# The first expert's list and the end of the last expert, in a kernel of retention, eight experts and a rational two-layer block

## The chip, the core and the metric

The kernel runs on one core of a Trainium2 chip. The metric is the device time of one execution in microseconds. Engines are called as in the profile: PE is TensorE's products and PEld its weight loads, DVE is VectorE, ACT is ScalarE, POOL is GpSimd, SP is SyncE, which here only issues transfers.

## The reference, cut to what matters

Three stages follow each other. N = 4608 tokens (8 x 576), width 512 (8 heads x 64), 8 experts of inner width 1024, a last block of inner width 2048.

```python
ret = (q @ k.T / 8) * gamma[h] ** (i - j), causal;   x = ret @ v        # retention, 8 heads
do_compute = x @ w_skip > 0                                             # router
e_idx = argmax(x[do_compute] @ w_gate);  gate_w = softmax value of e_idx
x[tokens of e] += gate_w * (relu(x @ w1[e]) @ w2[e])                    # eight experts
h = x @ w_in                                                            # last block
P = a0 + a1*h + a2*h*h + a3*h*h*h
Q = 1 + |b0|*|h| + |b1|*h*h
out = (P / (Q + 1e-6)) @ w_out
```

## The kernel before, in words

Products run with operands split in a high and a low part (two float32r halves), three products for one; 12 products of 512 columns make one inner tile. Work is written in an order by hand: under `manual_schedule` each engine gets its instructions in the order in which the Python code emits them, and waits only for semaphores. The change moves code, so it moves instructions on every engine.

*Stage 1* (to about 235 us) does the retention and the router over 36 token tiles. The router writes, by indirect DMA on POOL, each token's number into the list of its expert in DRAM (`XI`), and a list `PM` that puts 1024 tokens in an order in which the first 512 hold none of the last expert's. Then comes a branch (`spill`, L596) for experts with more than 336 tokens, which isn't taken here; all engines pass it.

*Stage 2* (to about 530 us) goes through the eight experts. `lists` (L661) loads an expert's list into `idx`, `gather` (L676) fetches its tokens' rows from `Z` in DRAM by three indirect DMAs, `turn_e` transposes them on PE (L694), with the high part cast on ACT (L695) and the low part on DVE (L696). Expert e has eight steps: steps 0 to 3 are `up` (L722, 24 products of 336 columns each), steps 4 to 7 are `down` (L743, 18 output products each). After the last one DVE adds the sums to the tokens (L748), and `scatter` (L759) writes them back to `Z` on POOL. `feed` moves the weights through 8 slots: SP loads them into one of three `raw` buffers (L112, L116, and L110 for the last block's second matrix, slots 64 to 71), ACT casts the high part (L127), DVE subtracts the low part (L131). The load for slot s waits until the low part of slot s - 3 has been read. Ahead of the first expert, PE runs 20 products whose result isn't used (`spin`, L501).

*Stage 3* works on nine blocks of 512 tokens. A block's rows come by `fetch` (SP; block 0 and block 1 by indirect DMAs of POOL, `fetch_at`, L685), are transposed (`turn_f` for block 0, `turn_b` for the others, one PSUM buffer for the latter), and then run through 16 steps. Step n has: `head` (12 products L774 on PE into one of three PSUM buffers `h`; five operations on ACT, L781 to L785; two on POOL, L786 and L787), `quot` (three on DVE: L798 product with `h`, L799 reciprocal, L800 the quotient), `parts` (ACT cast L805, POOL low part L806) and `back` (12 products L907 into the block's four output sums). In the steady order, step n emits head n, parts n - 2, quotient n, back n - 4. In steps 5 to 8 of block 0 the last two weight slots are split in halves (`part_rest`, L941 and L942). The four buffers `gt` that hold the split quotients begin with two `raw` buffers, those of the last weights.

What sets the order around the change: the list's load is in ACT's queue; in the last expert the block's transposes stand in steps 5 and 6, heads 0 and 1 behind the third output group, and the last expert's scatter behind head 2.

Of the kernel before, what the change touches and what calls it, by code (L numbers as in the profile page):

```python
# [17 lines left out]
N, DM = B * S, H * D  # L18
# [13 lines left out]
NBLK = N // TB  # L32
NF2 = F2 // P
LAG = 4
SPIN = (10, 20)
NQ = 2 * TB // P
OOB = 1 << 20
TINY = 2.0 ** -15
# [39 lines left out]
def body(nc, tc, a, out):  # L78
# [577 lines left out]

    gap = nblk[0:1, E + 1:E + 2]

    def lists(e0, e1):
        for e in range(e0, e1):  # L660
            nc.scalar.dma_start(out=idx[:, e], in_=XI[e * RR:e * RR + NC3 * P, :].rearrange("(c p) t -> p c t", p=P))  # L661
        if e1 == E:
            nc.scalar.dma_start(out=pidx, in_=PM.rearrange("(c p) t -> p c t", p=P))

# [14 lines left out]
                bounds_check=N - 1, oob_is_err=False), "get", ["put"])  # L679


    def fetch_at(j):
        nc.gpsimd.memset(gap, 0)
        for c in range(TB // P):
            ins = nc.gpsimd.indirect_dma_start(  # L685
                out=d2[:, c, :], out_offset=None, in_=Z[:, :],
                in_offset=bass.IndirectOffsetOnAxis(ap=pidx[:, j * (TB // P) + c, 0:1], axis=0),
                bounds_check=N - 1, oob_is_err=False)
            if j == 0:
                apart(ins, "first", [])  # L690
# [101 lines left out]
    def head(j, f):  # L792
        el[j, f] = act(j, f)

    def quot(j, f):
        ps, p, q = el[j, f]
        V = nc.vector
        V.scalar_tensor_tensor(out=ps, in0=p, scalar=ab[:, 1:2], in1=ps, op0=ALU.add, op1=ALU.mult)  # L798
        V.reciprocal(out=q, in_=q)  # L799
        V.scalar_tensor_tensor(out=p, in0=ps, scalar=ab[:, 0:1], in1=q, op0=ALU.add, op1=ALU.mult)  # L800

    def parts(j, f):
        p = el.pop((j, f))[1]
# [4 lines left out]

    order = ExitStack()
    order.enter_context(tc.manual_schedule())  # L810
    spin(ps_h.tile([P, DM], F32, tag="h", name="spin"), win[0][:, 0], SPIN[1])
    lists(0, 1)
    gather(0)
    feed(4, 4)
    for c in range(NC3):
        turn_e(0, c)
    feed(0)
    while nxt["raw"] < 6:
        load_raw(nxt["raw"])
# [3 lines left out]
    for e in range(E):  # L823
        for i in range(8):
            s = 8 * e + i
            if i == 1:
                gather(e + 1) if e + 1 < E else fetch_at(0)
            if s == 3:
                lists(2, E)
            if i < 4:  # L830
                up(e, i)
                if i == 0 and e > 0:
                    scatter(e - 1)
            else:
                if e + 1 == E and i in (5, 6):
                    if i == 5:
                        cvx.close()
                        el_p = ctx.enter_context(tc.tile_pool(name="el", bufs=2, reuse_waits="tile"))
                        pq.append(tuple(el_p.tile([P, TB], F32, name=nm + "0", bufs=1) for nm in "pq"))
                    turn_f(2 * i - 10)  # L840
                    turn_f(2 * i - 9)
                elif e + 1 < E and i < 4 + NC3:
                    turn_e(e + 1, i - 4)
                down(e, i - 4)
                if e + 1 == E and i == 6:
                    feed(NSLOT - 2)
                    feed(0)
                    head(0, 0)
                    quot(0, 0)
                    head(0, 1)  # L850
            feed(5 + s + min(max(s - 58, 0), 3), NSLOT - 2)
            K = 2 * (NCV - NCA) + 2
            for ph in range(*(min(max(x - 6, 0) * K // 54, K) for x in (s, s + 1))):
                n = NCA + ph // 2
                if ph % 2 == 0:
                    cv(conv_load, n + 1, NCA, NCV)
                    cv(conv_abs, n, NCA, NCV)
                    cv(conv_words, n, NCA, NCV)
                    cv(conv_hi, n - 1, NCA, NCV)
                else:  # L860
                    cv(conv_add, n, NCA, NCV)
                    cv(conv_lo, n - 1, NCA, NCV)
    quot(0, 1)
    gt = [pool["raw"].tile([P, 1024], F32, tag="raw", name="raw")[:, :].bitcast(F32R)
          .rearrange("p (h t) -> p h t", h=2) for _ in range(2)]
    parts(0, 0)
    head(0, 2)
    scatter(E - 1)
    quot(0, 2)
    mo.close()  # L870
    right.close()

# [11 lines left out]
    os = {}  # L884

    def fetch(j):
        if j == 1:
            fetch_at(j)
            return
        for c in range(NTB):  # L890
            r = j * TB + c * P
            nc.sync.dma_start(out=d2[:, c, :], in_=Z[r:r + P, :])
# [53 lines left out]
    for n in range(3, M + LAG):  # L946
        if n < M:
            j, f = steps[n]
            if f == 5 and j + 1 < NBLK:
                fetch(j + 1)  # L950
            at = TB_AT if j else (11, 12, 13, 14)
            if f in at and j + 1 < NBLK:
                turn_b((j + 1) * NTB + at.index(f))
            head(j, f)
            for x in late:
                put_at(*x)
            late.clear()
        if n < M + 2:
            parts(*steps[n - 2])
        if n < M:  # L960
            quot(j, f)
        if 5 <= n < 5 + len(rest):
            part_rest(n - 5)
        if n >= LAG:
            back(*steps[n - LAG])
# [32 lines left out]
```

## Time and profile before

| what | us |
|---|---|
| three runs: median (lowest, highest) | 1346.33 (1341.47, 1347.14) |
| the profiled execution | 1344.77 |
| its span, first to last instruction | 1342.8 |
| TensorE busy in the span | 1297.7 (97%) |
| VectorE, ScalarE, GpSimd busy | 1074.2, 793.5, 786.9 |
| mean granted TensorE clock, as a share of the full one | 0.984 |
| one indirect gather on POOL, busy, and the pause after it | 1.0 and 0.3 |

A matmul that waits on a pipeline still counts as busy, so the share of 97% says little; the waits of PE and the granted clock in each stretch say where time can go. The clock has two levels here, 1.0 (2.4 GHz) and 0.5 (1.2 GHz). In the timeline an entry is a run of instructions of one line; the number in brackets is the idle time of its engine before it and what ended that wait.

### The profile page before, as it was taken

To read this page: it belongs to the slowest core of one execution; us is meant where nothing else is said; L and a number is where in the kernel's file an instruction comes from. 1 tells how busy PE (TensorE), PEld (TensorE's weight loads), DVE (VectorE), ACT (ScalarE), POOL (GpSimd) and SP (SyncE) were. 2 spreads that over 40 slices of the span, in tenths; PEclk is the share of its full clock that TensorE was granted. 3 is DMA by queue.
4 is the path that set the end of the run, shared out by engine and by line. 5 is a ranking of instruction groups with operands and counts; after the bars stand their busy time and mean duration, and the time that the engine had idled before them with its cause. 6 is when DMAs were issued, how large, how long until landed. Compare 5 with 4: busy or idle time off the path is not lost.

```text
span 1342.8 us, 20351 instructions
## 1 busy us (share of the span) xinstructions
PE 1297.7 (97%) x7615; PEld 1087.7 (81%) x7615; DVE 1074.2 (80%) x1140; ACT 793.5 (59%) x1379; POOL 786.9 (59%) x666
## 2 busy tenths in 40 slices
PE   8999998799999998989999999999999999999998
PEld 6887887688888886868888888888888888888886
DVE  3786886367777776888798898888888888888885
ACT  3564664244444445666676777666676676766764
POOL 3466565223333332866777777676666666666774
PEclk8999999799999999989999999999999999999999
DMA  9999993367666764100200101001010010010000
GB/s 213 251 212 210 245 250 92 92 201 220 217 222 223 233 222 145 52 1 1 63 1 29 35 1 63 0 6 59 1 63 1 1 63 1 23 40 1 32 1 31
DMA packets 160555, 128.16 MB, mean 95 GB/s; under 512 B 87930, under 2 KB 127610, under 8 KB 160448
## 3 DMA queue, kind: packets, MB, share of 16 engines
q1 hardware_dynamic: 149248, 111.71, 30.4%
q0 software_dynamic: 6272, 13.73, 3.0%
q10 hardware_dynamic: 4928, 1.34, 0.5%
q8 instruction: 61, 1.00, 0.3%
q14 instruction: 46, 0.38, 0.1%
HBM read 99.35 MB, written 28.93 MB: 96 GB/s over the span
## 4 chain that ended last, share of the span: by engine, by line
PE 84%; DVE 6%; issue 3%; DMA 3%; POOL 2%; ACT 1%; SPq 1%; POOLq 0%; ACTq 0%; DVEq 0%
PE h L774 27%; PE o L907 27%; PE y L743 9%; PE h L722 8%; PE xp L373 2%; PE ot L335 2%; PE ot L330 2%; PE sc L314 2%; PE t L694 2%; DVE q L799 2%; PE st L352 1%; PE tp L291 1%; PE tp L304 1%; DMA c<-in_moe_w_out 1%; DMA lk<-in_k 1%
## 5 line engine op out<-in xcount | busy, mean ns | idle before, releaser
L799 DVE RECIPROCAL q<-q 128x512 f32<-128x512 f32 x142 | 476.0, 3352 | 74.1 <-POOL q L787 74.1
L786 POOL TENSOR_TENSOR p<-p,h 128x512 f32<-128x512 f32 x142 | 183.9, 1295 | 164.3 <-ACT p L782 164.2
L774 PE MATMUL h<-d,wi 128*128 128x512 f32 x960 | 236.0, 396 | 5.3 <-DVE d L800 3.0
L787 POOL TENSOR_TENSOR q<-q,s 128x512 f32<-128x512 f32 x142 | 184.1, 1297 | 66.0 <-ACT s L785 59.3
L774 PEld LDWEIGHTS h<-d,wi 128*128 128x128 f32 x960 | 181.2, 190 | 43.9 <-DVE d L800 3.5
L781 ACT COPY h<-h 128x512 f32<-128x512 f32 x144 | 85.1, 591 | 211.9 <-PE h L774 211.9
L907 PE MATMUL o<-w,raw 128*128 128x512 f32 x864 | 207.8, 389 | 0.1
L907 PE MATMUL o<-w,g 128*128 128x512 f32 x864 | 207.6, 389 | 0.0
L907 PEld LDWEIGHTS o<-w,raw 128*128 128x128 f32 x864 | 162.2, 188 | 34.2 <-POOL raw L806 0.5
L907 PEld LDWEIGHTS o<-w,g 128*128 128x128 f32 x864 | 162.0, 188 | 34.0 <-POOL g L806 0.2
L774 PE MATMUL h<-xb,wi 128*128 128x512 f32 x768 | 186.5, 392 | 0.0
L774 PEld LDWEIGHTS h<-xb,wi 128*128 128x128 f32 x768 | 143.0, 188 | 29.4
L743 PE MATMUL y<-w,hr 128*128 128x512 f32 (+1 forms) x576 | 139.2, 397 | 0.0
L782 ACT ACTIVATE p<-h,ab 128x512 f32<-128x512 f32 x142 | 111.4, 785 | 45.1 <-POOL g L806 28.4
L722 PE MATMUL h<-d,w 128*128 128x336 f32 x768 | 121.9, 320 | 1.8 <-DVE hr L727 1.3
L722 PEld LDWEIGHTS h<-d,w 128*128 128x128 f32 x768 | 120.4, 191 | 3.4 <-DVE hr L727 1.8
L743 PEld LDWEIGHTS y<-w,hr 128*128 128x128 f32 (+1 forms) x576 | 98.9, 175 | 29.6
L785 ACT ACTIVATE s<-s,ab 128x512 f32<-128x512 f32 x144 | 119.2, 828 | 0.0
L798 DVE SCALAR_TENSOR_TENSOR h<-p,ab,h 128x512 f32<-128x512 f32 x142 | 106.0, 747 | 14.9 <-POOL p L786 14.9
L800 DVE SCALAR_TENSOR_TENSOR p<-h,ab,q 128x512 f32<-128x512 f32 x142 | 106.7, 751 | 5.0
L185 POOL TENSOR_TENSOR cr<-cr,cy 128x256 f32<-128x256 f32 x32 | 24.8, 775 | 136.8 <-DVE cr L178 96.1
L127 ACT CAST w<-raw 128x1024 fp32r<-128x1024 f32 x70 | 73.4, 1048 | 53.1 <-DMA raw<-in_moe_w 30.8
(129 smaller groups left out, 1844.5 us busy)
## 6 DMA issues: line engine op xcount, KB each, us to landing
raw<-in_moe_w SPq DMA_DIRECT2D x62, 512.0 KB, 4.2
Z<-xs SPq DMA_DIRECT2D x36, 256.0 KB, 4.3
lk<-in_k SPq DMA_DIRECT2D x32, 256.0 KB, 5.5
lv<-in_v SPq DMA_DIRECT2D x32, 256.0 KB, 5.9
c<-in_moe_w_in SPq DMA_DIRECT2D x16, 512.0 KB, 6.4
c<-in_moe_w_out SPq DMA_DIRECT2D x31, 256.0 KB, 4.6
d<-Z SPq DMA_DIRECT2D x28, 256.0 KB, 3.7
out<-d SPq DMA_DIRECT2D x27, 256.0 KB, 2.4
```

What stands on the lines that cost most here:

```text
L722: nc.tensor.matmul(out=ps, lhsT=w[:, pw, k, ff * P:(ff + 1) * P], rhs=xp[e][:, px, k, :], start=(n == 0), stop=(n == 11))
L743: nc.tensor.matmul(out=ys[e][c][0:cnt[c]], lhsT=h[:, ph, c * P:c * P + cnt[c]], rhs=w[:, pw, ff, :], start=(i == 0 and ff == 0 and j == 0) ...
L774: nc.tensor.matmul(out=ps, lhsT=w[:, pw, k, o:o + P], rhs=xb[j][:, px, k, :], start=(n == 0), stop=(n == 11))
L781: S.copy(out=h, in_=ps)
L782: S.activation(out=p, in_=ps, func=A.Identity, scale=ab[:, 3:4], bias=ab[:, 2:3])
L785: S.activation(out=s, in_=s, func=A.Identity, scale=ab[:, 5:6], bias=ab[:, 6:7])
L786: G.tensor_tensor(out=p, in0=p, in1=h, op=ALU.mult)
L787: G.tensor_tensor(out=q, in0=q, in1=s, op=ALU.add)
L798: V.scalar_tensor_tensor(out=ps, in0=p, scalar=ab[:, 1:2], in1=ps, op0=ALU.add, op1=ALU.mult)
L799: V.reciprocal(out=q, in_=q)
L800: V.scalar_tensor_tensor(out=p, in0=ps, scalar=ab[:, 0:1], in1=q, op0=ALU.add, op1=ALU.mult)
L907: nc.tensor.matmul(out=os[j][c], lhsT=g[:, pg, c * P:(c + 1) * P], rhs=w[:, pw, f % 2, :], start=(f == 0 and i == 0), stop=(f == NF2 - 1 a ...
```

## The change

1. The first expert's list is loaded from SP's queue (`lists(0, 1, nc.sync)`), and three of the unused products follow each of the first expert's three transpose groups.
2. In the last expert the transposes of block 0 move from steps 5 and 6 to steps 4 and 5, head 0 goes ahead of the third output group (step 6), and the last eight weight casts are spread: the step's own `feed` no longer runs ahead, and the rest follows quotient 1. The scatter comes before quotient 1, head 2 ahead of the last parts.
3. The quotient is cut in two: `quot_a` is L798, `quot_b` the reciprocal and the last operation. In step n, `quot_b` of n - 1 is emitted ahead of head n and `quot_a` of n after parts. What is emitted between them on DVE (a weight half, the low part of a transpose) now lies between the two.
4. The four gathers of block 1 go one by one into steps 5 to 8, and its transposes into steps 9, 11, 13 and 14 instead of 11 to 14.

```diff
-SPIN = (10, 20)
+SPIN = (10, 20, 3)
...
-    def lists(e0, e1):
+    def lists(e0, e1, eng=nc.scalar):
         for e in range(e0, e1):
-            nc.scalar.dma_start(out=idx[:, e], in_=XI[...])
+            eng.dma_start(out=idx[:, e], in_=XI[...])
...
-    def fetch_at(j):
-        nc.gpsimd.memset(gap, 0)
-        for c in range(TB // P):
+    def fetch_at(j, cs=range(TB // P)):
+        if cs[0] == 0:
+            nc.gpsimd.memset(gap, 0)
+        for c in cs:
...
-    def quot(j, f):
+    def quot_a(j, f):
+        ps, p, q = el[j, f]
+        nc.vector.scalar_tensor_tensor(out=ps, in0=p, scalar=ab[:, 1:2], in1=ps, op0=ALU.add, op1=ALU.mult)
+
+    def quot_b(j, f):
         ps, p, q = el[j, f]
         V = nc.vector
-        V.scalar_tensor_tensor(out=ps, in0=p, scalar=ab[:, 1:2], in1=ps, op0=ALU.add, op1=ALU.mult)
         V.reciprocal(out=q, in_=q)
         V.scalar_tensor_tensor(out=p, in0=ps, scalar=ab[:, 0:1], in1=q, op0=ALU.add, op1=ALU.mult)
+
+    def quot(j, f):
+        quot_a(j, f)
+        quot_b(j, f)
...
-    spin(ps_h.tile([P, DM], F32, tag="h", name="spin"), win[0][:, 0], SPIN[1])
-    lists(0, 1)
+    lists(0, 1, nc.sync)
+    idle = ps_h.tile([P, DM], F32, tag="h", name="spin")
+    spin(idle, win[0][:, 0], SPIN[1])
     gather(0)
     feed(4, 4)
     for c in range(NC3):
         turn_e(0, c)
+        spin(idle, win[0][:, 0], SPIN[2])
...
-                if e + 1 == E and i in (5, 6):
+                if e + 1 == E and i in (4, 5):
                     if i == 5:
                         cvx.close()
...
-                    turn_f(2 * i - 10)
-                    turn_f(2 * i - 9)
+                    turn_f(2 * i - 8)
+                    turn_f(2 * i - 7)
+                elif e + 1 == E and i == 6:
+                    head(0, 0)
...
                 down(e, i - 4)
                 if e + 1 == E and i == 6:
-                    feed(NSLOT - 2)
-                    feed(0)
-                    head(0, 0)
                     quot(0, 0)
                     head(0, 1)
-            feed(5 + s + min(max(s - 58, 0), 3), NSLOT - 2)
+            feed(5 + s, NSLOT - 2)
...
+    scatter(E - 1)
     quot(0, 1)
+    feed(NSLOT - 2)
+    head(0, 2)
+    feed(0)
...
     parts(0, 0)
-    head(0, 2)
-    scatter(E - 1)
-    quot(0, 2)
+    quot_a(0, 2)
...
     def fetch(j):
-        if j == 1:
-            fetch_at(j)
-            return
...
-            if f == 5 and j + 1 < NBLK:
+            if j == 0 and 5 <= f < 5 + NTB:
+                fetch_at(1, (f - 5,))
+            if f == 5 and 0 < j < NBLK - 1:
                 fetch(j + 1)
-            at = TB_AT if j else (11, 12, 13, 14)
+            at = TB_AT if j else (9, 11, 13, 14)
             if f in at and j + 1 < NBLK:
                 turn_b((j + 1) * NTB + at.index(f))
+        if n <= M:
+            quot_b(*steps[n - 1])
+        if n < M:
             head(j, f)
...
         if n < M:
-            quot(j, f)
+            quot_a(j, f)
```

The change moves instructions; three places show it. The first is PE's queue at the first expert (`t` are its tokens' transposes, `spin` the unused products, `h<-d_4313,w` its up products). Before:

```order
L596 UNCONDITIONAL_BRANCH x2
L501 MATMUL spin<-wi_78 128x512 x20
L694 MATMUL t<-ident,d_4314 128x128 x8
L694 MATMUL t<-ident,d_4314 128x80 x4
L722 MATMUL h<-d_4313,w 128x336 x96
```

and in the changed kernel:

```order
L596 UNCONDITIONAL_BRANCH x2
L501 MATMUL spin<-wi_78 128x512 x20
L695 MATMUL t<-ident,d_4314 128x128 x4
L501 MATMUL spin<-wi_78 128x512 x3
L695 MATMUL t<-ident,d_4314 128x128 x4
L501 MATMUL spin<-wi_78 128x512 x3
L695 MATMUL t<-ident,d_4314 128x80 x4
L501 MATMUL spin<-wi_78 128x512 x3
L723 MATMUL h<-d_4313,w 128x336 x96
```

Three products now stand behind each transpose group; the list's load, which was ScalarE's first instruction after the branch, is SyncE's.

The second is PE's queue at the last expert's end (`y` its output products, `h<-d_4313,wi` heads, `o` backs, `t<-ident,d_4314` the transposes of block 0). Before, from the end of the up products:

```order
L722 MATMUL h<-d_4313,w 128x336 x96
L743 MATMUL y<-w,hr 128x512 x6
L743 MATMUL y<-w,hr 80x512 x3
L743 MATMUL y<-w,hr 128x512 x6
L743 MATMUL y<-w,hr 80x512 x3
L694 MATMUL t<-ident,d_4314 128x128 x8
...
L694 MATMUL t<-ident,d_4314 128x128 x8
...
L774 MATMUL h<-d_4313,wi_78 128x512 x24
L743 MATMUL y<-w,hr 128x512 x12
L743 MATMUL y<-w,hr 80x512 x6
L774 MATMUL h<-d_4313,wi_79 128x512 x24
```

and in the changed kernel:

```order
L723 MATMUL h<-d_4313,w 128x336 x96
L695 MATMUL t<-ident,d_4314 128x128 x8
...
L695 MATMUL t<-ident,d_4314 128x128 x8
...
L775 MATMUL h<-d_4313,wi_78 128x512 x12
L744 MATMUL y<-w,hr 128x512 x6
L744 MATMUL y<-w,hr 80x512 x3
L744 MATMUL y<-w,hr 128x512 x6
L744 MATMUL y<-w,hr 80x512 x3
L775 MATMUL h<-d_4313,wi_78 128x512 x12
L744 MATMUL y<-w,hr 128x512 x12
L744 MATMUL y<-w,hr 80x512 x6
L775 MATMUL h<-d_4313,wi_79 128x512 x24
```

The transposes now come straight after the up products, and heads 0 and 1 have an output group behind each.

The third is DVE's queue there (`w<-raw,w` is the low part of a weight slot, `ysb` the last expert's sums, then quotients 0 and 1). Before:

```order
L131 TENSOR_TENSOR w<-raw,w 128x1024 x3
L798 SCALAR_TENSOR_TENSOR h<-d_4314,ab,h 128x512
L799 RECIPROCAL d_4314<-d_4314 128x512
L800 SCALAR_TENSOR_TENSOR d_4314<-h,ab,d_4314 128x512
L748 SCALAR_TENSOR_TENSOR ysb<-y,idx,xg_4336 128x512 x2
L748 SCALAR_TENSOR_TENSOR ysb<-y,idx,xg_4336 80x512
L798 SCALAR_TENSOR_TENSOR h<-d_4314,ab,h 128x512
```

and in the changed kernel:

```order
L803 RECIPROCAL d_4314<-d_4314 128x512
L804 SCALAR_TENSOR_TENSOR d_4314<-h,ab,d_4314 128x512
L131 TENSOR_TENSOR w<-raw,w 128x1024
L749 SCALAR_TENSOR_TENSOR ysb<-y,idx,xg_4336 128x512 x2
L749 SCALAR_TENSOR_TENSOR ysb<-y,idx,xg_4336 80x512
L131 TENSOR_TENSOR w<-raw,w 128x1024
L798 SCALAR_TENSOR_TENSOR h<-d_4314,ab,h 128x512
L803 RECIPROCAL d_4314<-d_4314 128x512
L804 SCALAR_TENSOR_TENSOR d_4314<-h,ab,d_4314 128x512
L131 TENSOR_TENSOR w<-raw,w 128x1024 x3
L798 SCALAR_TENSOR_TENSOR h<-p_7068,ab,h 128x512
```

Five weight parts that stood ahead of quotient 0 now stand between the quotients and behind quotient 1.

## Rows read from the trace of the kernel before

**Rows 1.** Busy time by stretch: length, PE, PEld, DVE, ACT, POOL, PEclk, DMA, GB/s
```profile
252.00:258.00 6.00, 5.48 (x23) 5.10 (x22) 3.01 (x4) 1.39 (x4) 0.00 (x0) 0.50 0.61 195
500.60:609.20 108.60, 96.34 (x418) 76.87 (x417) 87.08 (x66) 65.04 (x107) 61.04 (x50) 0.95 0.21 68
609.20:1324.00 714.80, 714.80 (x3206) 591.29 (x3205) 629.86 (x414) 486.45 (x834) 502.83 (x396) 1.00 0.07 23
```

**Rows 2.** Chain of waits ahead of the first expert: start us, us, what
```profile
235.62 5.33 DMA XI<-rowt,sx
240.94 4.72 DMA idx<-XI
```

**Rows 3.** By line: L661's issues (ns min/median/max) and landing, L391's issues
```profile
L661 ACTq DMA_DIRECT2D idx<-XI x8: 375/504/3159, 240.9 to 272.6; - x8
DMA to landing us min/median/max: 2.8/3.8/4.3
...
L391 SPq DMA_DIRECT2D Z<-xs x36: 319/414/1918, 30.2 to 231.7; - x36
```

**Rows 4.** Timeline of PE, first expert: start, us, [idle before <- releaser]
```profile
250.78 0.63 PE L694 MATMUL t<-ident,d 128*128 128x128 f32 x4 [3.17 <-issue]
253.83 17.14 PE L722 MATMUL h<-d,w 128*128 128x336 f32 x96 [0.52 <-ACT d L695]
```

**Rows 5.** Chain of waits, whole span: another expert, its outputs, one head
```profile
288.91 14.72 PE h L722 x96
304.06 4.18 PE y L743 x18
609.39 2.72 PE h L774 x12
```

**Rows 6.** Timeline of PE, last expert's end
```profile
511.47 1.25 PE L694 MATMUL t<-ident,d 128*128 128x128 f32 x8 [1.46 <-DVE d L696]
519.12 5.74 PE L774 MATMUL h<-d,wi 128*128 128x512 f32 x24 [2.23 <-ACT d L695]
537.54 4.61 PE L774 MATMUL h<-d,wi 128*128 128x512 f32 x12 [3.04 <-DVE d L800]
```

**Rows 7.** Timeline of ACT and DVE: head 0's first, fifth operation, quotient 0
```profile
522.23 0.59 ACT L781 COPY h<-h 128x512 f32<-128x512 f32 x1 [2.22 <-PE h L774]
524.43 0.83 ACT L785 ACTIVATE s<-s,ab 128x512 f32<-128x512 f32 x1
...
526.68 3.35 DVE L799 RECIPROCAL d<-d 128x512 f32<-128x512 f32 x1 [1.01 <-POOL d L787]
530.07 0.75 DVE L800 SCALAR_TENSOR_TENSOR d<-h,ab,d 128x512 f32<-128x512 f32 x1
```

**Rows 8.** Timeline of DVE, POOL, ACT: parts, sums, one cast; landing of L110
```profile
519.82 3.48 DVE L131 TENSOR_TENSOR w<-raw,w 128x1024 fp32r<-128x1024 f32 x3
530.73 2.05 DVE L748 SCALAR_TENSOR_TENSOR ysb<-y,idx,xg 128x512 f32<-128x512 f32 x3
...
531.55 1.29 POOL L806 TENSOR_TENSOR raw<-d,raw 128x512 fp32r<-128x512 f32 x1 [1.62 <-ACT raw L805]
...
518.95 1.06 ACT L127 CAST w<-raw 128x1024 fp32r<-128x1024 f32 x1
...
DMA to landing us min/median/max: 3.7/3.8/4.8
```

**Rows 9.** Timeline of PE at block 0's second turn
```profile
588.38 1.12 PE L694 MATMUL t<-ident,d 128*128 128x128 f32 x4 [4.92 <-DVE xb L696]
589.14 4.83 PE L774 MATMUL h<-d,wi 128*128 128x512 f32 x12
```

**Rows 10.** Timeline of ACT and DVE at block 1's first turn
```profile
658.34 0.60 ACT L695 CAST d<-t 128x512 fp32r<-128x512 f32 x1
663.41 0.68 DVE L696 TENSOR_TENSOR d<-t,d 128x512 fp32r<-128x512 f32 x1
```

More of the change, by code (lines that the diff above doesn't have):

```diff
@@ L657, in body @@
     gap = nblk[0:1, E + 1:E + 2]
-    def lists(e0, e1):
+    def lists(e0, e1, eng=nc.scalar):
         for e in range(e0, e1):
-            nc.scalar.dma_start(out=idx[:, e], in_=XI[e * RR:e * RR + NC3 * P, :].rearrange("(c p) t -> p c t", p=P))
+            eng.dma_start(out=idx[:, e], in_=XI[e * RR:e * RR + NC3 * P, :].rearrange("(c p) t -> p c t", p=P))
         if e1 == E:
```

## The prediction

> **What bounds the kernel now.** I read the busy time by stretch first [rows 1]. From 609.2 us to 1324 us TensorE is busy for all 714.80 us at the full granted clock: there the two-layer block runs at its floor, one group of 12 products every 2.72 us [rows 5], and nothing done on another engine can shorten it. What is left lies ahead of it, in two places. In the stretch 500.6 to 609.2, the end of the last expert and the first of nine token blocks, TensorE is busy for 96.34 of 108.60 us, part of it at half clock. The other place is the hand-over to the first expert. In the chain of waits [rows 2] the last routing write is issued at 235.62 and takes 5.33 us, the first expert's list takes 4.72 us more, the gathers follow, and the experts' products start at 253.83 [rows 4].
>
> The stretch in numbers. I call the 12 products of L774 that open step n "head n", the 12 of L907 that close it for step n "back n", and L798 to L800 "quotient n". From 500.6 to the start of head 15 at 609.2 (609.39 in the chain [rows 5], whose pieces lag the timeline by 0.16) TensorE does four groups of 18 output products at 4.18, eight groups of transposes at about 0.45, 15 heads and 11 backs at 2.72: 16.7 + 3.6 + 70.7 = 91.0 us. It took 108.6, so 17.6 us are lost. The rows name most of it: waits of 1.46, 2.23 and 3.04 [rows 6] and of 4.92 us [rows 9], and two heads at half clock, 4.61 and 4.83 us where a lone head takes about 2.9, another 3.7. The 4.92 us wait is a transpose group that needs VectorE to have read the group before it.
>
> **The change part by part.** *First list on SyncE.* On ScalarE this list's issue takes 3.16 us; the eight lists there have a median of 0.50, and SyncE's writes of Z one of 0.41 [rows 3]. The list waits for the routing write in both versions. On SyncE nothing is queued ahead of it, and behind it stand only weight loads whose buffers are not yet free. A list lands 2.8 to 4.3 us after its issue [rows 3], against 4.72 in the chain: the gain is between 0 (the issue is as slow there too) and 1.9 us. I take the median landing, 3.8: 0.9 us.
>
> By the Trainium skill ("DMA: Bandwidth & Descriptors", section "Issuing engines are not separate DMA queues") all issuing engines feed the same 16 DMA engines, and another issuer saves only the time to initiate a transfer, which it calls usually small. By that rule this term is nothing and the whole sum comes out at 1331.9 us; the 3.16 us row says that the initiation is not small here.
>
> *Nine products between the transposes.* After each of the three transpose groups TensorE runs three products of 512 columns: 0.23 us each at full clock (2.72/12), 0.40 at half (4.83/12) [rows 5, 9]. Before, TensorE stood 3.17 us ahead of the first transposes and 0.52 us ahead of the experts' products; the clock was at 0.50 from 252 to 258 [rows 1, 4], and the first expert's products took 17.14 us where another expert's take 14.72 [rows 4, 5]: 2.4 us to win. With the list 0.9 us earlier the idle time shrinks to 2.3 us. Two ends: if the clock stays up, the nine take 2.0 us, nearly all of it while the next gather lands, I estimate 0.2 on the path, and the place gives -0.9 + 0.2 - 2.4 = -3.1 us. If it falls, the nine and the transposes run at half speed and put about 3.0 us on the path while the 2.4 are won: -0.3; with a slow list as well, +0.6. The row nearest to 2.3 us idle is the 2.23 us wait, after which heads 0 and 1 ran at full speed (5.74 for 24 [rows 6]). I take -3.1.
>
> *New order at the last expert's end.* The transposes of block 0 move ahead of the first output group, so that their casts lie under 4.18 us of products; heads 0 and 1 stand between the output groups; the casts of the last weights move behind. TensorE then runs without a wait: 0.9 + 4.18 + 0.9 + 4.18 from 500.6, head 0 at 510.8 (before 519.12 [rows 6]), outputs, head 1 at 517.7, outputs to 524.6, heads 2 and 3 to 530.1. The 1.46 and 2.23 us waits go. Two others are late next.
>
> Head 4 needs the "h" buffer of head 1 back, which is free when quotient 1 is done. An unhindered head gives its quotient 9.0 us after its last product: head 0 ended at 519.12 + 2.72 = 521.84, its L800 at 530.82 [rows 6, 7]. So quotient 0 is done at 522.5; VectorE then has one weight part (1.17, a third of 3.48), the three sums (2.05) and another part [rows 8] to 526.9, and quotient 1 (0.67 + 3.3 + 0.75 [rows 7]) to 531.6. Head 4 waits 1.5 us and ends at 534.3.
>
> Back 0 needs the buffer in which the last weights lie. The load of slot 69 is issued when VectorE has read slot 66, at 526.9, and lands 3.8 us later [rows 8], at 530.7; ScalarE's cast of it (1.06 [rows 8]) now stands ahead of head 2's five operations (3.03 [rows 7]), which end at 534.8. VectorE's three remaining parts (3.48) end at 535.1. Then a cast to 535.7, and on POOL the sum of head 2 to 536.2 and the low part for back 0 (1.29 [rows 8]) to 537.5. Back 0 starts there, after a wait of 3.2 us. Quotient 2 lets head 5 start at 540.4. From there ten heads, ten backs and four transpose groups, 54.4 + 1.8 = 56.2 us, reach head 15 at 596.6, 12.6 us earlier than 609.2. The 3.2 us wait is nearest to the 3.04 us one, after which a head took 4.61 us [rows 6], so I charge 1.9 us for a half-speed spell (4.83 - 2.9): 10.7 us. With a landing of 4.8 us [rows 8] and a second spell it is 7.8; without a spell 12.6.
>
> *Spread gathers, split quotient, other turn steps.* One gather of about 1.3 us per step instead of four in one keeps POOL at 5.2 us a step, under the 5.44 of a head and a back. The four weight halves and the transposes' low parts now go ahead of the reciprocal, into the time in which VectorE would wait for POOL. With turns at 9, 11, 13 and 14 each low part is read before the next transposes come: the 4.92 us wait and its half-speed head are in the 12.6 already. In the later blocks TensorE is never short, so the split is worth nothing there; I cost it at 0. The cover is VectorE's slack, 5.44 less 4.7 of quotient; what it costs if the cover is gone is the fourth rival.
>
> The sum against the profiled execution's 1344.77 us (span 1342.8): 1344.77 - 3.1 - 10.7 = 1331.0. The median of the three runs, 1346.33, is 1.6 above that execution, and they span 5.7 us, so about 3 us either way stay open.
>
> **Rivals.** *The first place gives nothing.* SyncE's issue is as slow as ScalarE's, the clock falls, the nine products run at half speed on the path: +0.6 instead of -3.1, 1334.7 us. For it: the slow issue was the first after the branch, and SyncE comes from the same branch. Against it: SyncE's queue has been in use all along.
>
> *The stall at the turns stays.* If VectorE comes to the turns as late as before, since the four weight halves still put about 5.7 us of work into each of steps 5 to 8, 4.92 + 1.9 = 6.8 us come back: 1337.8 us. Against it: the halves now fill VectorE's waits, and a step lies between the first three turns.
>
> *The wait only moves.* ScalarE and VectorE lose as much to slots 66 to 69 between heads 1 and 2 as the order wins, because the loads follow each other, each released by the part three slots before: about 1343 us, no change. Against it: only two of these loads are issued after 522 in the walk above.
>
> *Slower: the reciprocal waits for ScalarE's cast.* In a turn the low part now stands ahead of the reciprocal. In the trace a cast ends at 658.94 and its low part runs only at 663.41 [rows 10], so the cast's lateness was hidden. If the reciprocal stands for the cast and the low part (0.60 + 0.68 [rows 10]) in each of the 32 turns while POOL's sum is ready, that is 32 x 1.28 = 41 us: 1372. It decides where the delay exceeds VectorE's 0.7 us of slack in a step. Against it: the slack builds up again in the steps between turns.
>
> **How the numbers follow.** Forecast 1331 with chance 0.57; its own range is 1328 to 1337, from 4 to 0 at the first place (4 if the list lands after 2.8 us) and 12.6 to 7.8 at the second. First place empty 0.20, stall stays 0.10, wait only moved 0.08, slower 0.05. The range 1326 to 1339.5 takes in the first two, most of the third and the runs' spread. About 0.5%, 6.7 us off 1346.33, is what a measurement of this kernel can tell from no change; that is at 1339.6. Faster: 0.57 + 0.20 + 0.07 = 0.84; same: 0.08 + 0.03 = 0.11; slower 0.05.
>
> **What would show it.** Right: SyncE's list issue under 0.6 us; the first expert's products in about 14.8 us at full clock; head 0 near 510.8, less what the first place wins; waits of TensorE only ahead of head 4 and back 0; no wait of 4.9 us at the turns; from head 15 on the same 714.8 us. Wrong: a SyncE issue of 3 us; the clock at 0.50 after the nine products; a longer wait for slots 68 and 69; a reciprocal that waits for a low part in the later blocks.

## The result, and the profile after

The changed kernel takes 1329.75 us (median of 6 runs, 1327.56 to 1331.80) against 1343.12 us for the kernel before (6 runs, 1339.78 to 1347.14): ratio 0.9905, 95% interval 0.9888 to 0.9922, so 13.4 us faster. I had forecast 1331.0 us. The profiled execution took 1331.80 us with a span of 1330.0, 12.8 us less than the span before.

Stage 1 begins and ends the same in both kernels, but its length differs by up to 5 us from execution to execution (the unused products begin at 240.86 us in the trace before, between 240.98 and 245.84 in the others here). So I count two ways that leave it out. *Way A* goes from the start of the 20 unused products to the end of the last expert's up products, *way B* from there to head 15. Before they are 500.67 - 240.86 = 259.8 and 609.23 - 500.67 = 108.6 us; after, 497.59 - 241.21 = 256.4 and 596.54 - 497.59 = 98.95. Way A gives 3.4 us, way B 9.6, the rest nothing.

Way B has two pieces, parted by the start of head 6. From the end of the up products to head 6 it takes 550.17 - 500.67 = 49.5 us before and 545.63 - 497.59 = 48.0 after: the new order at the last expert's end gives 1.5 us in these two executions (0.1 to 2.6 with the other traces of this order, by their half-speed spells). From head 6 to head 15 it takes 59.06 us before and 50.91 after: 8.15 us, most of the gain, lie in block 0's later steps.

The busy time by stretch of the changed kernel (columns as in [rows 1]):

```profile
252.00:258.00 6.00, 6.00 (x40) 5.75 (x39) 3.27 (x5) 2.20 (x4) 0.00 (x0) 1.00 0.64 219
497.59:596.54 98.95, 95.08 (x418) 76.26 (x416) 86.49 (x66) 64.59 (x107) 63.63 (x50) 0.97 0.24 75
596.54:1311.34 714.80, 714.80 (x3206) 591.34 (x3205) 630.92 (x415) 486.52 (x834) 502.82 (x396) 1.00 0.07 23
```

From 252 to 258 us TensorE has its full clock now (0.50 in [rows 1]); the last line is the same 714.80 us as before. The first list's issue, by line (ns, min/median/max), and TensorE's timeline at the first expert:

```profile
L661 SPq DMA_DIRECT2D idx<-XI x1: 407/407/407, 241.5 to 241.5; - x1
...
241.21 7.53 PE L501 MATMUL spin<-wi 128*128 128x512 f32 x20 [6.08 <-PEq L596]
249.42 0.63 PE L695 MATMUL t<-ident,d 128*128 128x128 f32 x4 [0.68 <-issue]
249.80 0.95 PE L501 MATMUL spin<-wi 128*128 128x512 f32 x3
...
252.76 14.93 PE L723 MATMUL h<-d,w 128*128 128x336 f32 x96
```

The issue takes 0.41 us where ScalarE's took 3.16 [rows 3]; TensorE stands 0.68 us ahead of the first transposes, not 3.17 [rows 4], and the up products take 14.93 us, not 17.14. TensorE's timeline at the last expert's end:

```profile
507.68 2.89 PE L775 MATMUL h<-d,wi 128*128 128x512 f32 x12
...
529.10 4.47 PE L775 MATMUL h<-d,wi 128*128 128x512 f32 x12 [1.99 <-DVE d L804]
534.24 0.50 PE L915 MATMUL o<-w,raw 128*128 128x512 f32 x1 [0.68 <-ACT raw L813]
535.94 4.07 PE L915 MATMUL o<-w,raw 128*128 128x512 f32 x11 [1.20 <-POOL raw L814]
539.81 3.27 PE L775 MATMUL h<-d,wi 128*128 128x512 f32 x12
```

Head 0 starts 11.4 us earlier than in [rows 6]. From there on only head 4 and back 0 wait, 1.99 and 0.68 + 1.20 us, and the 4.92 us at the turn [rows 9] are gone: to its last product TensorE never stops again. Half speed lies on head 4, back 0 and part of head 5 (4.47, 4.07, 3.27 us): the granted clock is 0.64 from 529.1 to 533.5 us, 0.65 from 535.9 to 540 and 0.91 from 540 to 543.

### The profile page after: what moved, and what is told of

The parts are those of the page before. It is cut to its first block, busy times and chain, and to the rows that moved or that the text cites. A ratio compares the mean times of both kernels' runs of the same rounds, so it can differ in the third digit from the quotient of the medians.

```text
span 1330.0 us, 20367 instructions
## 1 busy us (share of the span) xinstructions
PE 1293.9 (97%) x7624; PEld 1085.1 (82%) x7624; DVE 1075.1 (81%) x1140; ACT 793.4 (60%) x1379; POOL 789.4 (59%) x666
## 4 chain that ended last, share of the span: by engine, by line
PE 77%; issue 2%; DVE 1%; POOL 1%; DMA 1%; ACT 0%; SPq 0%; ACTq 0%; POOLq 0%; DVEq 0%
PE o L915 29%; PE h L775 29%; PE y L744 9%; PE h L723 8%; PE t L695 2%; PE spin L501 1%; DMA c<-in_moe_w_out 1%; DVE w L131 0%; DVE d L803 0%; POOL raw L814 0%; POOL Z L760 0%; POOL p L787 0%; DVE ysb L749 0%; POOL d L788 0%; POOL d L787 0%
## 5 line engine op out<-in xcount | busy, mean ns | idle before, releaser
L798 DVE SCALAR_TENSOR_TENSOR h<-p,ab,h 128x512 f32<-128x512 f32 x142 | 106.0, 746 | 8.8 <-POOL p L787 8.8
L785 ACT ACTIVATE q<-h,ab 128x512 f32<-128x512 f32 x142 | 99.3, 699 | 0.0
```

The lines of the kernel that those rows point to most:

```text
L785: S.activation(out=q, in_=ps, func=A.Abs, scale=ab[:, 4:5])
L798: nc.vector.scalar_tensor_tensor(out=ps, in0=p, scalar=ab[:, 1:2], in1=ps, op0=ALU.add, op1=ALU.mult)
```

## The experiments

Each is timed against the kernel before in several rounds on one chip; the ratio has its 95% interval in brackets. The median of the kernel before was 1343 to 1349 us on these chips, so ratios are compared, not times. Ways A and B are read from the profiled execution.

**1. The first place alone** (the kernel before with `lists(0, 1, nc.sync)` and `SPIN[2] = 3` after each transpose group) **and the rest alone.** The second, against the changed kernel:

```diff
-    lists(0, 1, nc.sync)
+    lists(0, 1)
...
         turn_e(0, c)
-        spin(idle, win[0][:, 0], SPIN[2])
```

Expected of the first place alone:

> The kernel before with the first place's part of the change alone: the list on SyncE's queue and three products after each transpose group. Theory (the places act by themselves): the gain of the trace after, where the experts' products start 8.2 us behind the unused products' start plus 3.3 us instead of 13.0, and take 14.9 us: 3.4 us earlier at the end of the last expert's up products, so about 1339.7 us against 1343.1, ratio 0.9975; the stretch from the last expert's first output group to head 15 stays at 108.6 us. Rival (the first place gives nothing by itself, all came from the second): ratio 1.000.

Expected of the rest alone:

> The changed kernel with the list back on ScalarE and without the nine products: what is left is the last expert's end, split quotient, spread gathers, other turn steps. Theory: 9.7 us of the 13.4 come from here, 1333.5 us, ratio 0.993; ScalarE's issue of the first list takes about 3.2 us again, the first expert's products 17.1 us; from the last expert's outputs to head 15 98.95 us as in the changed kernel. Rival (the stretch depends on when the first expert starts): the stretch is over 101 us and the ratio above 0.995.

Measured: ratio 0.9982 (0.9966 to 0.9998), way A 256.4, way B 108.6; and ratio 0.9927 (0.9906 to 0.9948), way A 259.5, way B 99.75, ScalarE's issue of the first list 3.24 us, the first expert's products 16.54 us (17.1 expected). The places add up: each has its own gain. Way B without the first place is 0.8 us longer than in the changed kernel, which is within what this way varies by: 97.8 to 100.3 us in the six traces that have the changed kernel's order there (the changed kernel twice, this run, the two of experiment 2 and that of experiment 4).

**2. The first place taken apart:** the list on SyncE without the nine products, and the nine products with the list on ScalarE.

> The changed kernel without the nine products between the first expert's transposes; the list stays on SyncE. I count from the start of the unused products to the last expert's first transposes of block 0 or its first output group, whichever is first: 259.8 us before, 256.4 in the changed kernel. Theory (the nine products keep the clock up): the first expert's products start about 0.2 us earlier than in the changed kernel but take about 17 us at half clock, 258.5 us. Rival (the shorter wait alone, 0.7 to 1.7 us, keeps the clock up, the nine do nothing): 14.9 us, 256.3 us.

> The changed kernel with the first list back on ScalarE's queue, with the nine products. The same count. Theory (the nine keep the clock up whatever the list does): the first transposes come 1.7 us later than in the changed kernel, the first expert's products take 14.9 us: 258.0 us. Rival (a wait of 2.5 to 3.2 us ahead of the transposes lets the clock fall, and then the nine run at half speed on the path): 259.5 to 260.5 us, no better than before.

TensorE's timeline with the list alone:

```profile
241.56 6.69 PE L501 MATMUL spin<-wi 128*128 128x512 f32 x20 [6.20 <-DVEq L596]
249.77 0.63 PE L695 MATMUL t<-ident,d 128*128 128x128 f32 x4 [1.52 <-issue]
...
252.66 16.38 PE L723 MATMUL h<-d,w 128*128 128x336 f32 x96 [0.52 <-ACT d L696]
```

and with the nine products alone:

```profile
242.06 7.67 PE L501 MATMUL spin<-wi 128*128 128x512 f32 x20 [6.12 <-DVEq L596]
251.82 0.63 PE L695 MATMUL t<-ident,d 128*128 128x128 f32 x4 [2.10 <-issue]
...
255.13 14.94 PE L723 MATMUL h<-d,w 128*128 128x336 f32 x96
```

| from the start of the unused products, us | transposes | up products | these take | way A |
|---|---|---|---|---|
| neither (before; the rest alone) | 9.92; 10.10 | 12.97; 12.80 | 17.14; 16.54 | 259.8; 259.5 |
| list on SyncE | 8.21 | 11.10 | 16.38 | 257.8 |
| nine products | 9.76 | 13.07 | 14.94 | 258.3 |
| both (changed kernel) | 8.21 | 11.55 | 14.93 | 256.4 |

The timed ratios, 0.9911 (0.9882 to 0.9939) and 0.9918 (0.9890 to 0.9946), are too wide to part these cases; the ways do it. The list brings the transposes 1.7 us forward (9.92 to 8.21) and way A 1.9 to 2.0 us (259.8 to 257.8, 258.3 to 256.4). The nine products take the half-speed time from the up products, in both rows. With the list alone the granted clock is 0.54 from 252.6 to 256 us and 1.00 from there on; with the nine alone it is 1.00 from the transposes to the end of the up products. So the theory of the clock holds; what it brings is 1.4 us (257.8 to 256.4). Way A with the list alone is 0.7 us under what was expected, since half speed ended sooner than before.

**3. Which part removed the 4.92 us wait at the turn?** Once with the old turn steps and gathers, once with the quotient in one piece:

```diff
-            if j == 0 and 5 <= f < 5 + NTB:
-                fetch_at(1, (f - 5,))
+            if j == 0 and f == 5:
+                fetch_at(1)
...
-            at = TB_AT if j else (9, 11, 13, 14)
+            at = TB_AT if j else (11, 12, 13, 14)
```

> The changed kernel with the turns of block 1 back at steps 11 to 14 and its four gathers together at step 5; the split quotient stays. Theory A (the split quotient by itself removed the 4.92 us wait, since the weight halves and the low parts now fill VectorE's waits): no turn wait over 1 us, 0 to 2 us for the four gathers in one, 1330 to 1332 us, against 1329.75 for the changed kernel. Theory B (the step between the turns removed it, as my prediction put it): a wait of 3 to 5 us at the second turn and a half-speed head behind it, 5 to 7 us, 1335 to 1337 us.

```diff
-    quot_a(0, 2)
+    quot(0, 2)
...
-        if n <= M:
-            quot_b(*steps[n - 1])
...
-            quot_a(j, f)
+            quot(j, f)
```

> The changed kernel with the quotient in one piece behind parts, as before, in the steps from 3 on; turns at 9, 11, 13, 14 and spread gathers stay. Theory A (the split is what block 0 needs): VectorE falls behind in steps 5 to 8, and TensorE waits 3 to 5 us at one of the turns, with a half-speed spell: 5 to 8 us, 1335 to 1338 us. Theory B (the turn steps do it): no wait over 1 us, 1330 us. In both the later blocks stay at 714.5 us, since TensorE is never short there.

Measured: ratio 0.9913 (0.9893 to 0.9932), way B 99.9, with the old turns; 0.9955 (0.9940 to 0.9971), way B 105.8, with the quotient in one piece. TensorE's timeline of the latter:

```profile
579.16 2.79 PE L915 MATMUL o<-w,g 128*128 128x512 f32 x11 [0.87 <-POOL g L814]
...
598.27 1.11 PE L695 MATMUL t<-ident,d 128*128 128x128 f32 x4 [4.25 <-DVE xb L697]
599.03 4.06 PE L775 MATMUL h<-d,wi 128*128 128x512 f32 x12
```

With the old turns no turn waits at all: head 6 to head 15 takes 50.91 us (546.83 to 597.74), exactly as in the changed kernel (545.63 to 596.54). In one piece it takes 58.65 (547.01 to 605.66): 7.7 us more, 4.25 of it the old wait on another turn. The split quotient did it: without it the new turn steps and spread gathers leave the wait, and with it they add nothing. Theory A.

Theory A also says why: VectorE's waits are filled. The traces show another effect of the split, the place of the low part in VectorE's queue. Two turns (the transposes of one group of tokens) on TensorE and their low parts on VectorE, first with the quotient in one piece, then with the split and the old turns:

```profile
587.88 0.66 PE L695 MATMUL t<-ident,d 128*128 128x128 f32 x4
597.53 0.68 DVE L697 TENSOR_TENSOR xb<-t,xb 128x512 fp32r<-128x512 f32 x1
...
579.96 0.60 PE L695 MATMUL t<-ident,d 128*128 128x128 f32 x4
583.82 0.68 DVE L697 TENSOR_TENSOR xb<-t,xb 128x512 fp32r<-128x512 f32 x1
```

In one piece the low part stands behind the whole quotient of the step before and begins 9.65 us after its transposes, while the next transposes, which need their buffer read, are due 5.9 us later where two turns stand in neighbouring steps. Split, it stands ahead of the reciprocal and the last operation (4.1 us) and begins 2.6 to 4.5 us after its transposes, in time even for the old turns. How much of the 7.7 us comes from this place and how much from filled waits no run separates.

**4. What does back 0 wait for?** The loads of slots 70 and 71 bring data that nobody reads there. Without them back 0's buffer comes free earlier:

```diff
-    feed(NSLOT - 2)
+    feed(NSLOT - 2, NSLOT - 2)
```

> The changed kernel without the loads of slots 70 and 71 into raw buffers, whose data nobody reads there: the first two quotient buffers then follow slots 68 and 69 instead of 69 and 71. Theory (back 0 waits for POOL, whose sum of head 2 ends at 534.63 in the changed kernel, not for the buffer): head 4 and back 0 start within 0.4 us of the changed kernel's, 0 to 0.5 us, ratio within 0.0005 of the changed kernel's. Rival (my prediction's walk: the last part of slot 69 on VectorE and the load hold back 0): back 0 starts 1.2 to 1.5 us earlier, up to 3 us with a shorter half-speed spell.

```profile
532.80 4.44 PE L775 MATMUL h<-d,wi 128*128 128x512 f32 x12 [1.99 <-DVE d L804]
537.03 0.60 PE L915 MATMUL o<-w,raw 128*128 128x512 f32 x1
539.64 4.03 PE L915 MATMUL o<-w,raw 128*128 128x512 f32 x11 [2.01 <-POOL raw L814]
```

These are TensorE's rows of it. The wait for ScalarE's cast (0.68 us) is gone and that for POOL grows by as much: way B is 98.95 us again. The ratio, 0.9889 (0.9864 to 0.9914), is too wide to tell half a microsecond; the way is not. The buffer isn't the limit; the low part on POOL is. POOL's products and VectorE's weight parts in the changed kernel, and the cast of slot 69 on ScalarE:

```profile
519.16 2.06 DVE L131 TENSOR_TENSOR w<-raw,w 128x1024 fp32r<-128x1024 f32 x1
...
528.96 4.58 DVE L131 TENSOR_TENSOR w<-raw,w 128x1024 fp32r<-128x1024 f32 x3
...
528.62 1.05 ACT L127 CAST w<-raw 128x1024 fp32r<-128x1024 f32 x1 [2.85 <-DMA raw<-WS]
...
530.92 1.54 POOL L787 TENSOR_TENSOR p<-p,h 128x512 f32<-128x512 f32 x1 [3.13 <-ACT p L783]
532.68 1.99 POOL L788 TENSOR_TENSOR q<-q,s 128x512 f32<-128x512 f32 x1 [0.22 <-ACT s L786]
534.63 1.25 POOL L814 TENSOR_TENSOR raw<-d,raw 128x512 fp32r<-128x512 f32 x1
```

Three parts take 4.58 us, where [rows 8] has 3.48, one part ahead of them 2.06, and two POOL products 1.54 and 1.99, where 1.30 is usual.

POOL itself came late. It stood 3.13 us for head 2's second operation on ScalarE; those operations stood behind the cast of slot 69, and ScalarE stood 2.85 us for that slot's load. The run without spare loads keeps this chain:

```profile
532.21 1.05 ACT L127 CAST w<-raw 128x1024 fp32r<-128x1024 f32 x1 [2.44 <-DMA raw<-WS]
```

So it rules out the buffer, not the load of slot 69.

**5. The last weight parts earlier.** In the changed kernel VectorE stands 6.96 us ahead of quotient 0 (to 513.34 us) and is then busy until 534.2 but for 1.0 us. So I moved parts of slots 65 to 68 ahead, in `feed`'s calls of the last expert's steps 4 to 7, and the sums stayed ahead of quotient 1; the load of slot 69 and its cast come earlier with them. The main hunk:

```diff
...
                 if e + 1 == E and i == 6:
-                    quot(0, 0)
+                    feed(5 + s + 1, NSLOT - 2)
+                    quot_a(0, 0)
+                    feed(0, NSLOT - 2)
+                    quot_b(0, 0)
+                    feed(NSLOT - 3, NSLOT - 2)
                     head(0, 1)
...
```

> The changed kernel with the last weight parts moved ahead: VectorE stood 7 us ahead of quotient 0 in the changed kernel while the buffers of slots 65 to 67 had landed; now the low parts of slots 64 to 66 stand ahead of quotient 0, that of 67 between its two halves, that of 68 ahead of the sums, that of 69 behind quotient 1, and no spare loads. Theory (VectorE's load between 513 and 534 us sets both waits): head 4 waits about 1 us instead of 2.0, back 0 not at all, head 5 about 0.8 us, and no or little half-speed time: 2.8 us of waits and about 3 us of half speed less, ratio 0.986. Rival (VectorE and POOL only slow each other elsewhere, or ScalarE's casts hold up head 0): no gain, ratio 0.990.

VectorE, POOL and TensorE in its timeline:

```profile
533.09 4.46 DVE L131 TENSOR_TENSOR w<-raw,w 128x1024 fp32r<-128x1024 f32 x1
537.47 0.74 DVE L798 SCALAR_TENSOR_TENSOR h<-p,ab,h 128x512 f32<-128x512 f32 x1
...
532.67 1.30 POOL L787 TENSOR_TENSOR p<-p,h 128x512 f32<-128x512 f32 x1
533.91 1.30 POOL L788 TENSOR_TENSOR q<-q,s 128x512 f32<-128x512 f32 x1
535.16 1.30 POOL L787 TENSOR_TENSOR p<-p,h 128x512 f32<-128x512 f32 x1
537.20 1.50 POOL L788 TENSOR_TENSOR q<-q,s 128x512 f32<-128x512 f32 x1 [0.74 <-ACT s L786]
...
533.22 3.04 PE L775 MATMUL h<-d,wi 128*128 128x512 f32 x12 [0.97 <-DVE d L804]
536.10 2.88 PE L924 MATMUL o<-w,raw 128*128 128x512 f32 x12
542.31 4.40 PE L775 MATMUL h<-d,wi 128*128 128x512 f32 x12 [3.33 <-DVE p L804]
```

Head 4 waits 0.97 us and back 0 not at all, as expected, but head 5 waits 3.33 instead of 0.8: way B 97.4, ratio 0.9890 (0.9864 to 0.9915) where 0.986 was expected. One part, 1.21 us elsewhere, took 4.46: it began 0.4 us into a POOL product and ended at 537.55, 1.1 us after POOL's first pause began (535.16 + 1.30 = 536.46). The products between stood back to back. The reciprocal and the other two quotient operations take the same time beside POOL as alone (3.34 to 3.36 and 0.74 to 0.76 us throughout the changed kernel).

VectorE doesn't always lose its turn so. In the kernel before, a weight half (0.68 us elsewhere) ran between two POOL products that stood back to back, and the second product took 1.74 us:

```profile
565.15 1.29 POOL L787 TENSOR_TENSOR q<-q,s 128x512 f32<-128x512 f32 x1 [0.47 <-ACT s L785]
565.96 1.03 DVE L942 TENSOR_TENSOR w<-xb,w 128x512 fp32r<-128x512 f32 x1
566.41 1.74 POOL L806 TENSOR_TENSOR raw<-p,raw 128x512 fp32r<-128x512 f32 x1
```

This is so for all four halves there. What decides who comes next stays open.

**6. The same, with no weight part beside POOL's products.** Parts 68 and 69 go between the halves of quotient 0, quotient 1 ahead of the sums; head 2 goes ahead of the scatter, and there are no spare loads. Two of the hunks:

```diff
...
+                elif e + 1 == E and i == 7:
+                    quot(0, 1)
...
                 if e + 1 == E and i == 6:
-                    quot(0, 0)
+                    feed(0, NSLOT - 2)
+                    quot_a(0, 0)
+                    feed(NSLOT - 3, NSLOT - 2)
+                    feed(NSLOT - 2, NSLOT - 2)
+                    feed(0, NSLOT - 2)
+                    quot_b(0, 0)
                     head(0, 1)
...
```

> As the run before with early weight parts, but no low part of a weight slot is left where POOL has products back to back, and quotient 1 stands ahead of the sums. In that run the low part of slot 69 took 4.46 us on VectorE while POOL ran three products without a pause, and ended 1 us after POOL's pause; elsewhere it takes 1.17. Theory (VectorE's low part and POOL's products shut each other out, and this is what stretches the parts in the changed kernel too, 4.58 us for three): all parts take 1.2 us but for those that begin within a POOL product; head 4 waits under 0.7 us, back 0 and head 5 under 1 us; the way from the last expert's first transposes to head 6 is 42 to 44 us instead of 48.0 (46.5 with early parts): ratio 0.985 to 0.987. Rival (the 4.46 us come from something else, such as its buffer or the write of the weights): a stretched part appears in the new place too, 46 us or more, ratio 0.989 or above.

```profile
514.57 2.63 DVE L131 TENSOR_TENSOR w<-raw,w 128x1024 fp32r<-128x1024 f32 x2 [0.57 <-ACT w L127]
517.12 3.34 DVE L803 RECIPROCAL d<-d 128x512 f32<-128x512 f32 x1
...
521.37 8.36 PE L775 MATMUL h<-d,wi 128*128 128x512 f32 x36
529.57 2.88 PE L924 MATMUL o<-w,raw 128*128 128x512 f32 x12
532.97 3.06 PE L775 MATMUL h<-d,wi 128*128 128x512 f32 x12 [0.52 <-issue]
```

Two parts take 2.63 us, heads 2 to 4 run through (8.36 us for 36), back 0 follows at once and head 5 waits 0.52 us. From the last expert's first transposes to head 6 it takes 41.8 us (48.0 in the changed kernel, 42 to 44 expected), way B is 92.8 us, and the ratio 0.9855 (0.9822 to 0.9889). No part is stretched by more than the rest of one POOL product, as the theory has it. But the run also takes the cast of slot 69 from ahead of head 2's operations and moves quotient 1, so it shows what the whole order gives and not how much of the 6.2 us is POOL and VectorE no longer stopping each other. Once more, with the changed kernel beside it on one chip:

> The changed kernel once more, beside the version with the parts off POOL's products, on one chip. By its earlier ratio, 0.9905 (0.9888 to 0.9922), some 13 us under the kernel before; the way from the unused products to the last expert's first transposes 256.4 us, from there to head 6 48.0 us or, with another half-speed spell, 47 to 49.

> The version with the parts off POOL's products once more. Theory: 6.25 us less than the changed kernel, as the way to head 6 says (41.8 against 48.0 us), so a ratio 0.0045 to 0.005 below it. Rival (the two ratios differed by the chips they were taken on): the same ratio within 0.002.

Measured: the changed kernel 1332.82 us, 0.9916 (0.9898 to 0.9935); this one 1327.49 us, 0.9871 (0.9848 to 0.9893), way B 100.3 and 93.0 us. It beats both kernels, the changed one by 5.3 us in the medians (6.25 expected); the intervals of the two ratios do not overlap.

**7. The half-speed spell.** Unused products fill the two waits of the changed kernel:

```diff
+            if n == 4:
+                spare = ps_t.tile([P, NP, P], F32, tag="t", name="t").rearrange("p k f -> p (k f)")
+                spin(spare, win[0][:, 0], 8)
             head(j, f)
...
+        if n == LAG:
+            spin(spare, win[0][:, 0], 16)
```

> The changed kernel with 8 unused products ahead of head 4 and 16 ahead of back 0, into an idle buffer: they fill TensorE's two waits and take nothing away from them. Theory (the half-speed spell of head 4, back 0 and head 5 comes from the waits, so a TensorE kept busy keeps its full clock): head 4 takes 2.9 us, back 0 2.8 after its wait, head 5 2.9; the way from the last expert's first transposes to head 6 falls from 48.0 to 44.5 to 45 us, 3 us less in all. Rival (the clock falls there for another reason, or the added products delay head 4 and back 0 by as much): 47.5 us or more.

```profile
528.09 1.98 PE L501 MATMUL t<-wi 128*128 128x512 f32 x8
530.24 3.02 PE L775 MATMUL h<-d,wi 128*128 128x512 f32 x12 [0.18 <-DVE d L804]
533.10 3.79 PE L501 MATMUL t<-wi 128*128 128x512 f32 x16
536.73 3.23 PE L915 MATMUL o<-w,raw 128*128 128x512 f32 x12
540.07 3.02 PE L775 MATMUL h<-d,wi 128*128 128x512 f32 x12
```

The granted clock is 1.00 from 530.2 to 543 us; back 0 takes 3.23 us because it waits for POOL inside. But head 6 comes only 1.1 us earlier (46.9 us from the first transposes, 48.0 in the changed kernel), not 3. Ratio 0.9887 (0.9858 to 0.9915). All eight traces of this order with the waits unfilled have a half-speed spell here and this one has none, so it is the waits that let the clock fall. My size was wrong. Half speed on head 4 lies in time that back 0 would have waited for POOL anyway: with the list alone (experiment 2) head 4 ran at half speed, and head 6 came after 46.9 us just the same.

## Why the prediction was right, point by point

- *List on SyncE: 0.9 us forecast, 1.7 measured* for the transposes (9.92 to 8.21 us). The 0.41 us issue was as said; the gain was taken too small, because I took the median landing, 3.8 us. In the run with the list alone the chain of waits has 2.52 us for this load, against 4.72 before; what follows it takes 1.1 us to the first gather in both, and SyncE's issue starts 0.5 us later than ScalarE's. So the first gather starts 4.2 us behind the unused products' start (245.44 us in the trace after), 5.9 before. The Trainium skill ("DMA: Bandwidth & Descriptors", section "Issuing engines are not separate DMA queues") calls what another issuer saves usually small; the runs disagree in size: 3.03 to 3.24 us of issue on ScalarE in every run with the list there, 0.41 on SyncE in every other. Why ScalarE's first issue is slow stays open.
- *Nine products: +0.2 on the path and -2.4 by the clock forecast; +0.1 to +0.45 and -1.4 to -2.2 measured* (table of experiment 2). I took the 2.4 from one execution: the same arrangement in experiment 1 has 16.54 us, not 17.14, and with the list earlier the half-speed time is shorter as well. The place came out at 3.4 us against 3.1 forecast because the two misses cancel, which is luck. The rival that the first place gives nothing is out.
- *Way B: 10.7 us forecast, 9.6 measured.* I put all of it under the new order. By the walk, head 6 starts at 545.8 us, or 547.7 with the spell's 1.9, 47.1 us behind the up products: 2.4 us of gain ahead of head 6 and 8.3 behind it. Measured are 1.5 and 8.15. Head 0 comes 10.1 us behind the up products, as walked (10.2). Head 4 waited 1.99 us (1.5 forecast).
- *Back 0: the right chain, 1.4 us short.* I walked from the load of slot 69 over ScalarE's cast and head 2's operations to POOL's sum and low part, 36.9 us behind the up products. The trace has this chain, and its low part was done at 38.3 (535.88 us). The step that failed is that all engines run at their undisturbed durations: a weight part beside POOL took 2.06 us, not 1.17, and so put off that load; the load took 4.2 us, not 3.8; POOL's sum beside a part took 1.99 us, not 1.30. VectorE's part of slot 69 and the buffer, which I also let back 0 need, were not what it waited for (experiment 4).
- *Half-speed spell: 1.9 us charged.* Experiment 7 gives 1.1 us against the changed kernel's trace, but the spell isn't the same each time: the runs with this order reach head 6 in 46.9 to 49.4 us from the first transposes (the 49.4 with 0.5 us lost at the transposes), and the one without a spell in 46.9. Where half speed fell on head 4 it lay beside the wait for POOL; where it fell on back 0 it cost up to 2.1 us.
- *The turn: right effect, wrong part.* I gave the lost 4.92 us to the turn steps, and said only that the weight halves and low parts go ahead of the reciprocal as well. Experiment 3 shows that the split does it, whichever turn steps are used: 7.7 of the 13 us. The rival "the stall stays" was priced at 6.8 us; without the split it is 7.7.
- *The slower rival* (the reciprocal waits for the cast in 32 turns) is out: 714.80 us from head 15 on, as before. The rival that the wait only moves was priced at 1343 us; without the 10.7 us the sum gives 1344.77 - 3.1 = 1341.7. Way B gained 9.6 us, so it is out too.

So 1344.77 - 3.4 - 9.6 = 1331.8, which is the profiled execution's time; the forecast was 0.8 us under it, by misses of 0.3 and 1.1 us of opposite sign. Both places and the end of the wait at the turn were foreseen rightly; that the total came so close is in part luck.

## What to carry to other kernels

Where an engine that works in order waits inside a sequence (here VectorE for POOL, between the quotient's first and second operation) and others wait for work behind that sequence, splitting it lets this work stand between: here 7.7 us, against 1.5 us for the new order at the last expert's end. Before walking along queues, look at how long the work that others wait for lies behind what releases it (9.65 us here) and how soon it is needed (5.9 us). A walk must use durations under contention: look in the trace for the same operation beside its neighbour, and place two-input VectorE work where POOL pauses. In these runs half speed cost only what wasn't covered by a wait behind it.

## What the runs showed of the hardware that I had not expected

- VectorE's weight part (two inputs in SBUF) and POOL's products stop each other, in whole instructions: 1.21 us alone, 4.46 us beside three POOL products, ending 1.1 us after POOL's pause began; a POOL sum 1.99 us instead of 1.30 behind a part. The Trainium skill ("SBUF — State Buffer", section "Who interferes with whom") says that a VectorE instruction with two SBUF inputs contends with a GpSimd instruction that reads SBUF, and calls the lock on the ports they share exclusive. The trace agrees. Between POOL products that stood back to back, VectorE's instruction was passed over twice in experiment 5, but got its turn with all four weight halves of the kernel before. Operations with one input in PSUM (L798, 0.74 to 0.76 us) aren't touched.
- A list of one expert issued first after the branch costs ScalarE's queue 3.0 to 3.2 us, later ones 0.50 (median); on SyncE the first one costs 0.41. The cause stays open.
- The half-speed spell behind the same two waits differs between executions: back 0's last 11 products took 2.79 us in two runs, 4.0 to 4.2 in three and 5.06 in three.
